# A convolution, mixer and MLP block on one core: the preparation in another order, and the last inverse transforms ahead of the mixing

## The chip, the cores and the metric

The kernel runs on one core of one Trainium2 chip. The time is that of one execution in microseconds on the device; the number given for a kernel is the median of its runs. The kernel before was run three times: 679.14 us, from 678.92 to 680.05. One further execution was profiled; its time is 679.21 us, and its span, from the first to the last instruction, 677.4 us. All times inside the kernel below come from that execution and count from the span's start.

## The reference, cut to what matters

The sequence has 2048 positions and 512 channels. A vector `c` gives six modulation vectors. Two residual parts follow, each behind a normalization and modulation:

```python
mod = (_silu(c) @ w_mod).reshape(c.shape[0], 6, 1, -1)      # sa, ca, ga, sb, cb, gb
h = _layernorm(x) * (1 + ca) + sa
x = x + ga * _A_ref(h, A_re, A_im, B_re, B_im, C_re, C_im, log_dt, Dskip)
h = _layernorm(x) * (1 + cb) + sb
x = x + gb * _B_ref(h, w1, w2, w3, w4)

# _A_ref: a state space convolution, 512 channels with 128 states each
logdA = exp(log_dt)[:, None] * (A_re + 1j * A_im)
K = einsum("dn,dnl,dn->dl", Cc, exp(logdA[:, :, None] * l), dB).real
y = irfft(rfft(pad(u)) * rfft(pad(K)))[:L] + u * Dskip

# _B_ref: token mixing by shifts, then an MLP
h = _gelu(_layernorm(x) @ w1);  hs = shifted(h, +1, -1, +2, -2) @ w2;  x1 = x + hs
return x1 + _gelu(_layernorm(x1) @ w3) @ w4
```

All is float32. Where the kernel multiplies matrices of full precision it splits a factor into a rounded part ("hi") and a rest ("lo") and adds up two or three products.

## The kernel before

The work of one core goes through five stages; their order on each engine is the order of the code, written out by hand (`manual_schedule`), and each engine works through its list in order. DMAs are issued by SP, GpSimd ("POOL") and at a few places by ScalarE ("ACT"), each queue in order as well.

**Preparation (0 to 31 us, lines 261 to 402).** From 128 x 512 inputs `ar`, `ai` (A), `br`, `bi`, `cr`, `ci` it makes the phases and weights of the kernel K. VectorE computes exp(log_dt) and silu's exponential in small operations (`exp_exact`, line 149, on `ld`, which holds log_dt and -c), then `la` and `tf`, the real and imaginary exponents (lines 319 to 322); `frac` takes a phase modulo one in two operations. `t64` is 64 times the phase (line 333). `hi` (line 309) is ScalarE's rounding into a slot of the tile `hilo`, `lo` (line 310) VectorE's rest. `place` (line 312) brings the rows of two such slots into matmul layout by TensorE and two ScalarE evictions: `TES` for the exponentials, `T0S` for the first phase. `parts` (line 360) does so for three pairs of slots into two PSUM tiles `px`, evicted as `T1S`. Lines 343 to 348 form the complex product C*B (`wr`, `wi`); lines 370 to 378 its phase by a quotient and ScalarE's Arctan; line 383 adds it to the phase, giving slots 4 and 5 of `hilo`. `exps(0, 0, 5)` (line 355) computes the first exponentials. GpSimd issues the loads of the tables PA, CE, C0, PB, C1 behind a copy that waits for `raw_ai` (line 286), then fills the constant tiles MG and ON (lines 291 to 299). SP loads the inputs, and behind VectorE's clearing of `DS` three modulation weights (1 MB each, `load_mod`) and two groups of u (1 MB each, `load_u`). At the end `wn` gets the weights of the states (lines 398 to 401). `mod_parts` (line 214) is the first half of a product c @ w_mod on TensorE with its eviction, `mod_sum` the second.

**Turns (31 to 205 us, lines 547 to 599).** For k = 0 to 31, `turns(k, cos)` (line 439) computes phases on TensorE into one of two PSUM tiles `xx`, 8 to 10 matmuls in pairs, and ScalarE takes the sine of them into `tr`. `products(k)` (line 459) multiplies them on VectorE with the exponentials, `burst(k)` (line 490) contracts over the states on TensorE. TensorE's order in step k: turns k+2, then burst k. The list `side` spreads other work over the steps: the statistics of u (`u_stats`), its normalization and its transform, and loads. For every fourth k the next exponentials come in between.

**Spectra (205 to 299 us, lines 1099 to 1152).** For sixteen steps the spectra of u and K are computed, multiplied, transformed back along one axis (`back`) and stored to a DRAM tile `ZT`.

**Last transforms and mixing (299 to 376 us, lines 1153 to 1294).** The second half of the channels has its last axis transformed from `ZT`. `load_inv(1, k)` loads block k, in halves or whole; `inv_half(1, g, i)` (line 725) is 16 small matmuls that yield one half of row group g, and returns the VectorE operation that adds it to the residual `X2`. The halves (3,1), (0,0), (3,0) and (0,1) need the blocks 0, 3, 4 and 7; (1,0), (1,1), (2,0), (2,1) the blocks 1, 2, 5 and 6. Those blocks live in a ring `ldp` of six buffers. Token mixing of eight groups of 256 rows begins with group 7: `first_stats`, `mix_mod1`, `mix_mod2` (VectorE and GpSimd), `mix_norm` (ScalarE), `transposed` (TensorE), `parts_of` (ScalarE evicts, VectorE forms the rest `nl`), `mix_half` (24 matmuls by W1, twice). `keep(n)` issues n matmuls whose result isn't used.

**Mixing and MLP (376 us to the end, `chan`).** TensorE works here without a break.

Of the kernel before, what the change touches and what calls it, by code (L numbers as in the profile page):

```python
# [82 lines left out]

def layouts(inp):
# [7 lines left out]
         "wm": np.ascontiguousarray(a("w_mod").reshape(4, 128, 6, 512).transpose(2, 1, 0, 3).reshape(6, 128, 2048)), "c": np.ascontiguousarray(a("c").reshape(4, 128).T),  # L92
         "ld": np.ascontiguousarray(perm(a("A_log_dt")).reshape(4, 128).T),
# [13 lines left out]
def body(ctx, tc, A):  # L107
# [15 lines left out]
    Y.dma_start(ident, A["ID"])  # L123
# [64 lines left out]
    T1S = ph.tile([128, 16, 128], F32R, name="T1S")  # L188
# [41 lines left out]
    ut = {}  # L230
# [33 lines left out]
    ld = pp.tile([128, 8], F32, name="ld")  # L264
    raw = {}
    PA = pp.tile([128, 2, 2, 128], F32R, name="PA")
    PB = pp.tile([128, 4, 4, 128], F32R, name="PB")
    cT = pp.tile([128, 4], F32, name="cT")
    cst = pp.tile([128, 512], F32, name="cst")
# [10 lines left out]
    with tc.manual_schedule():  # L280
        Y.dma_start(ld[:, :4], A["ld"])
        Y.dma_start(cT, A["c"])
# [8 lines left out]
        P.memset(cst, MAGIC)  # L291
        for r in (32, 96):
            P.memset(cst[r:r + 32], 1.0)
        P.tensor_copy(MG, cst)
        P.memset(cst[:, :384], 0.0)
        for i, (r, v) in enumerate(((0, 1.0), (0, -1.0), (32, 0.25))):
            for q in (r, r + 64):
                P.memset(cst[q:q + 1, i * 128:i * 128 + 128], v)
        P.tensor_copy(ON.rearrange("p a b -> p (a b)"), cst[:, :384])
# [33 lines left out]
        V.tensor_scalar(t64, tf, 64.0, None, op0=OP.mult)  # L333
        frac(t64, rr)
        hi(2, t64)
        place(TES, 6, PA)
        V.tensor_scalar(ex[:, 4:], ex[:, 4:], 1.0, None, op0=OP.add)
# [5 lines left out]
        V.tensor_mul(wr, cr, br)  # L343
# [21 lines left out]

        parts(range(4), 0)
        mp = [mod_parts(0)]
# [8 lines left out]
        V.tensor_mul(rc, rc, wi)  # L376
        V.scalar_tensor_tensor(t31, sg, 0.25, t31, op0=OP.mult, op1=OP.add)
        act(at0, rc, AF.Arctan)
        lo(2, t64)
        parts(range(4), 1)  # L380
# [3 lines left out]
        frac(at, t0)  # L384
        hi(4, at)
        mp[0]()
# [712 lines left out]
    with tc.manual_schedule():  # L1099
# [71 lines left out]
        for k, i in ((3, 1), (0, 0)):  # L1171
            load_inv(1, k, i, Y)
            load_inv(1, k + 4, i, Y)
# [141 lines left out]
```

## Time and profile before

| | |
|---|---|
| median of three runs | 679.14 us (678.92 to 680.05) |
| profiled execution: time, span | 679.21 us, 677.4 us |
| TensorE matmuls, busy | 633.1 us (93%) |
| VectorE busy | 496.8 us (73%) |
| ScalarE busy | 331.3 us (49%) |
| GpSimd busy | 118.4 us (17%) |
| first turns on TensorE | 31.67 us |
| first inverse half from the second `ZT` | 306.69 us |
| mean granted TensorE clock | 0.992 |

A timeline row reads: start in us, length in us, engine, line of the code, operation, written tile <- read tiles, shape, count, and in brackets the idle time of the engine just before and what ended it. PE is TensorE, PEld its weight loads, DVE VectorE, ACT ScalarE, POOL GpSimd, SPq the queue of SP. Line 115 is the helper through which every ScalarE operation goes, so ScalarE's rows are told apart by their tiles. Rows of the stage table have the busy time of each engine in a stretch, then the granted clock (1.00 is full), the busy share of the DMA engines and GB/s. Rows of the chain of waits have only start, length and what.

### The profile page before, as it was taken

The numbers are of one execution on the slowest core, as the hardware profiler recorded it, in microseconds if no ns is written. First come the engines' busy times: TensorE is split into PE (matmuls) and PEld (weight loads), VectorE is DVE, ScalarE is ACT, GpSimd is POOL, SyncE is SP. The second block draws the span as 40 slices with busy tenths as digits, with TensorE's granted clock in tenths as the row PEclk, the third lists the DMA queues.
The fourth block names the chain that finished last, engine by engine and source line by source line (L and its number), as shares of the span: only waits on it lengthen the run. The fifth ranks groups of instructions, "written<-read, shape, count | busy, mean of one in ns | idle before, by whom it ended". The sixth has DMA issues, their size and how long they took to land.

```text
span 677.4 us, 16876 instructions
## 1 busy us (share of the span) xinstructions
PE 633.1 (93%) x7195; PEld 507.1 (75%) x7195; DVE 496.8 (73%) x795; ACT 331.3 (49%) x505; POOL 118.4 (17%) x238
## 2 busy tenths in 40 slices
PE   1899999999999998968999999999999999999996
PEld 0456555665568877735889899898998989898895
DVE  7899999999996897997989777454674445363622
ACT  3978998898884665722446334022141213122121
POOL 4012212212207133203842002010010000000000
PEclk9999999999999999988999999999999999999999
DMA  8602274643838899966386010110100201010001
GB/s 306 287 2 75 75 229 107 202 124 80 296 64 311 289 372 354 364 209 197 110 268 237 1 60 4 49 46 16 48 31 25 70 16 48 1 62 1 1 32 31
DMA packets 50067, 86.42 MB, mean 128 GB/s; under 512 B 4676, under 2 KB 38472, under 8 KB 47400
## 3 DMA queue, kind: packets, MB, share of 16 engines
q1 hardware_dynamic: 45048, 60.97, 28.3%
q0 software_dynamic: 4624, 23.86, 9.7%
q8 instruction: 56, 0.92, 0.6%
q10 hardware_dynamic: 320, 0.52, 0.3%
q14 instruction: 19, 0.16, 0.1%
HBM read 59.12 MB, written 32.90 MB: 136 GB/s over the span
## 4 chain that ended last, share of the span: by engine, by line
PE 73%; DVE 4%; DMA 4%; issue 3%; ACT 2%; POOL 1%; SPq 0%; ACTq 0%; DVEq 0%; POOLq 0%
PE xx L448 7%; PE pm L840 7%; PE pm L838 7%; PE pm L837 7%; PE pa L957 6%; PE pa L956 6%; PE pa L964 6%; PE pk L679 4%; PE kp L498 4%; DMA ld<-ZT 3%; PE ph L894 2%; PE ph L895 2%; PE pu L426 2%; PE ph L897 2%; PE pz L701 2%
## 5 line engine op out<-in xcount | busy, mean ns | idle before, releaser
L115 ACT ACTIVATE gh<-pm 128x512 fp32r<-128x512 f32 (+1 forms) x48 | 26.9, 560 | 199.2 <-PE pm L840 199.2
L838 PE MATMUL pm<-nh,w3l 128*128 128x256 f32 (+1 forms) x352 | 85.6, 279 | 0.1
L837 PE MATMUL pm<-nh,w3h 128*128 128x256 f32 (+1 forms) x352 | 85.7, 278 | 0.0
L948 DVE TENSOR_TENSOR gl<-gf,gh 128x512 fp32r<-128x512 f32 (+1 forms) x48 | 30.8, 642 | 68.0 <-ACT gf L115 68.0
L956 PE MATMUL pa<-w4h,gh 128*128 128x512 f32 (+1 forms) x176 | 69.5, 395 | 0.0
L957 PE MATMUL pa<-w4l,gh 128*128 128x512 f32 (+1 forms) x176 | 68.9, 392 | 0.0
L838 PEld LDWEIGHTS pm<-nh,w3l 128*128 128x128 f32 (+1 forms) x352 | 65.2, 185 | 2.1 <-DVE w3l L757 0.5
L837 PEld LDWEIGHTS pm<-nh,w3h 128*128 128x128 f32 (+1 forms) x352 | 65.3, 186 | 1.4
L764 POOL TENSOR_TENSOR rs<-mv,eps_t 128x1 f32<-128x1 f32 (+1 forms) x39 | 11.0, 281 | 274.2 <-DVE mv L770 256.2
L840 PE MATMUL pm<-nl,w3h 128*128 128x256 f32 (+1 forms) x352 | 54.8, 277 | 0.1
L964 PE MATMUL pa<-w4h,gl 128*128 128x512 f32 (+1 forms) x176 | 48.0, 390 | 0.0
L449 PE MATMUL xx<-MG,ON 64*128 64x512 f32 x160 | 47.1, 390 | 0.0
L448 PE MATMUL xx<-MG,ON 64*128 64x512 f32 x160 | 47.0, 389 | 0.0
L840 PEld LDWEIGHTS pm<-nl,w3h 128*128 128x128 f32 (+1 forms) x352 | 46.6, 185 | 0.3 <-DVE nl L810 0.3
L900 DVE TENSOR_TENSOR h<-h,ph 128x512 f32<-128x512 f32 x16 | 11.0, 687 | 45.0 <-PE ph L897 45.0
L466 DVE SCALAR_TENSOR_TENSOR e<-tr,p 128x512 f32<-128x512 f32 x64 | 41.1, 683 | 0.4 <-ACT tr L115 0.4
L498 PEld LDWEIGHTS kp<-e,e 128*32 128x32 f32 x2048 | 30.1, 110 | 12.6 <-issue 7.9
L475 DVE TENSOR_TENSOR e<-tr,p 128x1024 f32<-128x1024 f32 x32 | 39.0, 1218 | 0.0
L476 DVE TENSOR_TENSOR e<-tr,m 128x1024 f32<-128x1024 f32 x32 | 39.0, 1218 | 0.0
L115 ACT ACTIVATE p<-xx 128x1024 f32<-128x1024 f32 (+1 forms) x40 | 37.5, 980 | 2.1 <-PE xx L252 0.5
L964 PEld LDWEIGHTS pa<-w4h,gl 128*128 128x128 f32 (+1 forms) x176 | 33.0, 188 | 7.1
L115 ACT ACTIVATE tr<-xx 128x1024 f32<-128x1024 f32 x32 | 33.0, 1030 | 9.7 <-PE xx L449 7.4
(241 smaller groups left out, 1709.7 us busy)
## 6 DMA issues: line engine op xcount, KB each, us to landing
VU<-vs SPq DMA_DIRECT2D x64, 128.0 KB, 3.4
ld<-VU SPq DMA_DIRECT2D x16, 512.0 KB, 8.7
ZT<-z POOLq DMA_DIRECT2D x30, 256.0 KB, 6.3
Dw<-in_w POOLq DMA_DIRECT2D x8, 688.0 KB, 4.7
xu<-in_u SPq DMA_DIRECT2D x4, 1024.0 KB, 11.9
KX<-in_x POOLq DMA_DIRECT2D x4, 1024.0 KB, 8.6
ld<-ZT SPq DMA_DIRECT2D x8, 512.0 KB, 10.4
win<-GD SPq DMA_DIRECT2D x32, 128.0 KB, 2.5
```

The source lines that it names most:

```text
L115: return S.activation(out, in_, f, bias=bias, scale=scale)
L448: T.matmul(x[:, :512], la, ma, start=(i == 0), stop=(i == len(ops) - 1))
L449: T.matmul(x[:, 512:], lb, mb, start=(i == 0), stop=(i == len(ops) - 1))
L466: V.scalar_tensor_tensor(e0[:, 1, a], tr[:, 1, 0], 1.0 - 2.0 * a, mg[:, a], op0=OP.mult, op1=OP.mult)
L475: V.tensor_mul(e0[:, 0], tr[:, 0, 0:1].to_broadcast([128, 2, 512]), mg)
L498: T.matmul(kp[32 * j:32 * j + 32, (k % 2) * 4 + g], e1[:, r, d], e0[:, r, :, d * 32:d * 32 + 32], start=(r == 0), stop=(r == 1), skip_grou ...
L837: T.matmul(p, wh[:, k, c], hi[k], start=(k == 0), stop=False)
L838: T.matmul(p, wl[:, k, c], hi[k], start=False, stop=False)
L840: T.matmul(p, wh[:, k, c], lo[k], start=False, stop=(k == 3))
L956: T.matmul(acc[i], gh[:m, e, s], W4h[:m, f], start=(f == 0), stop=False)
L957: T.matmul(acc[i], gh[:m, e, s], W4l[:m, f], start=False, stop=False)
L964: T.matmul(acc[i], gl[:m, e, s], W4h[:m, f], start=False, stop=(f == 10))
```

## The change

In the preparation:

- log_dt, c (twice) and four columns of constants come as one tile `lc` by one load, first in SP's queue; the load of `ident` goes from the very first place to behind u's first group.
- MG and ON are spread from these columns by ScalarE; GpSimd's fills and casts are gone.
- GpSimd's loads of the tables wait for `raw_ar` instead of `raw_ai`. A second copy on GpSimd waits for `wr`, then GpSimd (not VectorE) clears `DS`, behind which SP's large loads stand. Their order is now modulation 0, u 0, ident, modulation 1 and 2, u 1.
- `t64` is formed on ScalarE. The products `wr`, `wi` stand ahead of `frac(t64)`; the rest `lo(0)` and the place step for T0S go behind the quotient and Arctan; the first two `parts` are issued together; silu's three small operations go behind `frac(at)`.
- T1S is two tiles, each evicted by one operation. `mod_parts(1)` goes from ahead of the first turns to behind turns (0,1), `mod_sum` 0 and 1 behind turns (1,0), the transposes of `wn` ahead of turns (0,1).
- The statistics of u's first two blocks go from step 0 of the turns to the preparation, one ahead of and one behind the four operations on `wn`.

In the last transforms:

- Two of the first four loads of blocks go to ScalarE's queue.
- Blocks 1 and 5 of the second half get two buffers of their own (`xb`); the PSUM pool `psy` has four buffers instead of two.
- The halves (1,0), (1,1), (2,0) stand on TensorE right behind (0,1), (2,1) behind the addition of (0,0), all ahead of the transposes of group 7; `keep(14)` becomes `keep(4)`. The additions on VectorE keep their places.

```diff
+def constant_columns():
+    c = np.zeros((2, 64, 4), np.float32)
+    c[:, :32, 0], c[:, 32:, 0] = MAGIC, 1.0
+    c[:, 0, 1], c[:, 0, 2], c[:, 32, 3] = 1.0, -1.0, 0.25
+    return c.reshape(128, 4)
...
-    Y.dma_start(ident, A["ID"])
...
-    T1S = ph.tile([128, 16, 128], F32R, name="T1S")
+    T1S = [ph.tile([128, 8, 128], F32R, name=f"T1S{i}") for i in range(2)]
...
-        Y.dma_start(ld[:, :4], A["ld"])
-        Y.dma_start(cT, A["c"])
+        Y.dma_start(lc, A["ld"])
         for k in raw:
             Y.dma_start(raw[k].rearrange("p t n -> p (t n)"), A[k])
+        act(MG, lc[:, 12:13].to_broadcast([128, 512]))
+        act(ON, lc[:, 13:16, None].to_broadcast([128, 3, 128]))
         gate = pp.tile([128, 4], F32, name="gate")
-        P.tensor_copy(gate[:, 0:1], raw["ai"][:, 0, 0:1])
+        P.tensor_copy(gate[:, 0:1], raw["ar"][:, 0, 0:1])
...
-        P.memset(cst, MAGIC)
...
-        P.tensor_copy(ON.rearrange("p a b -> p (a b)"), cst[:, :384])
...
-        V.memset(DS, 0.0)
-        for j in range(4):
-            Y.dma_start(DS[32 * j:32 * j + 1], A["dk"][j:j + 1])
-        load_mod(0)
-        load_mod(1)
-        load_mod(2)
-        load_u(0)
-        load_u(1)
-        hi(0, tf)
-        lo(6, la)
-        V.tensor_scalar(t64, tf, 64.0, None, op0=OP.mult)
-        frac(t64, rr)
-        hi(2, t64)
-        place(TES, 6, PA)
-        V.tensor_scalar(ex[:, 4:], ex[:, 4:], 1.0, None, op0=OP.add)
-        V.reciprocal(ex[:, 4:], ex[:, 4:])
-        V.tensor_mul(scb, ex[:, 4:], cT)
...
+        hi(0, tf)
+        act(t64, tf, scale=64.0)
+        lo(6, la)
+        place(TES, 6, PA)
         V.tensor_mul(wr, cr, br)
...
+        P.tensor_copy(gate[:, 1:2], wr[:, 0:1])
+        P.memset(DS, 0.0)
+        for j in range(4):
+            Y.dma_start(DS[32 * j:32 * j + 1], A["dk"][j:j + 1])
+        load_mod(0)
+        load_u(0)
+        Y.dma_start(ident, A["ID"])
+        load_mod(1)
+        load_mod(2)
+        load_u(1)
...
-        lo(0, tf)
...
+        frac(t64, t0)
+        hi(2, t64)
         act(t31, tf, scale=31.5)
         exps(0, 0, 5)
         act(ws[:, :1], hpi, AF.Sin)
-        place(T0S, 0, PA)
...
-        parts(range(4), 0)
-        mp = [mod_parts(0)]
...
+        lo(0, tf)
         V.scalar_tensor_tensor(t31, sg, 0.25, t31, op0=OP.mult, op1=OP.add)
         act(at0, rc, AF.Arctan)
+        place(T0S, 0, PA)
         lo(2, t64)
-        parts(range(4), 1)
+        parts(range(4), 0, 1)
...
         frac(at, t0)
+        V.tensor_scalar(ex[:, 4:], ex[:, 4:], 1.0, None, op0=OP.add)
+        V.reciprocal(ex[:, 4:], ex[:, 4:])
+        V.tensor_mul(scb, ex[:, 4:], cT)
         hi(4, at)
-        mp[0]()
+        mp = [mod_parts(0)]
         lo(4, at)
         parts((0, 1), 2, 3)
         parts((2, 3), 2, 3)
-        mp.append(mod_parts(1))
         act(wn, at0, AF.Sin, scale=-1.0, bias=hpi)
-        T1v = T1S.rearrange("p (t v) n -> p v t n", v=4)
+        act(ws, at0, AF.Sin)
+        mp[0]()
         for i in range(2):
-            act(T1v[:, i], px[0].rearrange("p (v t n) -> p v t n", v=2, t=4)[:, i])
-        act(ws, at0, AF.Sin)
-        act(T1v[:, 2:], px[1].rearrange("p (v t n) -> p v t n", v=2, t=4))
-        mp[1]()
+            act(T1S[i].rearrange("p (t v) n -> p v t n", v=2), px[i].rearrange("p (v t n) -> p v t n", v=2, t=4))
+        ul[0] = ln_stats(ph, [ut[0][:, 0]], "l0")
...
+        ul[1] = ln_stats(ph, [ut[0][:, 1]], "l1")
...
         turns(0, 0)
-        turns(0, 1)
         wps = psu.tile([128, 512], F32, name="pu")
...
         act(WN, wps)
+        turns(0, 1)
+        mod_parts(1)()
+        turns(1, 0)
         ms = [mod_sum(n) for n in range(2)]
-        turns(1, 0)
...
-        psy = a2.enter_context(tp("psy", 2, space=PSUM, side="right"))
+        psy = a2.enter_context(tp("psy", 4, space=PSUM, side="right"))
+        xb = a2.enter_context(tp("xb", 2))
+        for k in (1, 5):
+            zis[1, k] = xb.tile([128, 4, 256], F32, name="xb")
...
         for k, i in ((3, 1), (0, 0)):
             load_inv(1, k, i, Y)
-            load_inv(1, k + 4, i, Y)
+            load_inv(1, k + 4, i, S)
...
         a01 = inv_half(1, 0, 1, psw, "pm")
-        keep(14)
+        a10 = inv_half(1, 1, 0, psy, "py")
+        a11 = inv_half(1, 1, 1, psy, "py")
+        a20 = inv_half(1, 2, 0, psy, "py")
+        keep(4)
...
         a00()
+        a21 = inv_half(1, 2, 1, psy, "py")
         mix_norm(7)
...
-        a10 = inv_half(1, 1, 0, psy, "py")
-        a11 = inv_half(1, 1, 1, psy, "py")
...
-        a20 = inv_half(1, 2, 0, psy, "py")
...
-        a21 = inv_half(1, 2, 1, psy, "py")
```

More of the change, by code (lines that the diff above doesn't have):

```diff
@@ L91, in layouts @@
          "x": np.ascontiguousarray(u.reshape(32, 4, 4, 2048).transpose(2, 1, 0, 3).reshape(4, 128, 2048)),
-         "wm": np.ascontiguousarray(a("w_mod").reshape(4, 128, 6, 512).transpose(2, 1, 0, 3).reshape(6, 128, 2048)), "c": np.ascontiguousarray(a("c").reshape(4, 128).T),
-         "ld": np.ascontiguousarray(perm(a("A_log_dt")).reshape(4, 128).T),
+         "wm": np.ascontiguousarray(a("w_mod").reshape(4, 128, 6, 512).transpose(2, 1, 0, 3).reshape(6, 128, 2048)), "ld": np.ascontiguousarray(np.concatenate([perm(a("A_log_dt")).reshape(4, 128).T] + [a("c").reshape(4, 128).T] * 2 +
+                                                   [constant_columns()], 1)),
          "dk": np.ascontiguousarray(a("A_Dskip").reshape(2, 2, 2, 64).transpose(0, 2, 1, 3).reshape(4, 128)),
@@ L228, in mod_sum @@
         return lambda: act(mods[k], m)
-    ut = {}
+    ut, ul = {}, {}
     def load_u(g):
@@ L263, in body @@
     pp = pr.enter_context(pool("prep"))
-    ld = pp.tile([128, 8], F32, name="ld")
+    lc = pp.tile([128, 16], F32, name="lc")
+    ld, cT = lc[:, :8], lc[:, 8:12]
     raw = {}
@@ L267, in body @@
     PB = pp.tile([128, 4, 4, 128], F32R, name="PB")
-    cT = pp.tile([128, 4], F32, name="cT")
-    cst = pp.tile([128, 512], F32, name="cst")
     hilo = pp.tile([128, 8, 512], F32R, name="hilo")
@@ L290, in body @@
         Y.dma_start(FU, A["FU"].rearrange("p (a b) -> p a b", a=2))
-        P.memset(cst, MAGIC)
[L292 to L298, printed above, removed]
-        P.tensor_copy(ON.rearrange("p a b -> p (a b)"), cst[:, :384])
         Y.dma_start(FK, A["FK"])
@@ L406, in body @@
     uv = a1.enter_context(pool("uv", bufs=2, reuse_waits="tile"))
-    ul = {}
     def u_stats(b):
@@ L442, in turns @@
         r1 = slice(64 - r0.start, 128 - r0.start)
-        l0, l1, c = T0S[r0, t], T1S[r1, t * 2 + k % 2], slice(k % 2 * 512, k % 2 * 512 + 512)
+        l0, l1, c = T0S[r0, t], T1S[t % 2][r1, t // 2 * 2 + k % 2], slice(k % 2 * 512, k % 2 * 512 + 512)
         x = psx.tile([128, 1024], F32, name="xx")
@@ L519, in body @@
     for i in range(16):
-        side[max(at(i) - 2, 0)].append(lambda i=i: u_stats(i))
+        if i > 1:
+            side[max(at(i) - 2, 0)].append(lambda i=i: u_stats(i))
         side[at(i)].append(lambda i=i: u_norm(i))
```

## The prediction

> **What bounds the kernel now.** I read the page first (chain of waits, busy shares), then the busy time by stages, then the timelines of the two places that the change touches. The page's chain by engine, and three rows by stage (length, busy time of TensorE, weight loads, VectorE, ScalarE, GpSimd, granted clock, DMA share, GB/s):
>
> ```profile
> PE 73%; DVE 4%; DMA 4%; issue 3%; ACT 2%; POOL 1%; SPq 0%; ACTq 0%; DVEq 0%; POOLq 0%
> ...
> 10.00:20.00 10.00, 4.73 (x11) 2.66 (x12) 9.59 (x18) 6.02 (x10) 3.48 (x10) 1.00 1.07 419
> ...
> 190.00:200.00 10.00, 10.00 (x188) 6.69 (x186) 10.00 (x12) 7.78 (x11) 0.00 (x0) 1.00 0.16 35
> ...
> 318.00:345.00 27.00, 25.76 (x238) 22.29 (x238) 25.34 (x51) 13.07 (x21) 18.04 (x49) 1.00 0.39 128
> ```
>
> The preparation (0 to 31 us) hangs on VectorE, 9.59 of 10 us busy, and at its end on ScalarE. In the turns (31 to 205) TensorE and VectorE are both full, so two chains run abreast and the later one counts. In the mixing (318 to 345) VectorE is busy 25.34 of 27. Later the work is TensorE's, so a shift that reaches it reaches the end.
>
> **The change, part by part: the preparation.** Timeline rows (start, length, what), VectorE and ScalarE:
>
> ```profile
> 1.65 0.43 SPq L282 DMA_DIRECT2D cT<-in_c  x1
> ...
> 3.33 0.17 DVE L301 TENSOR_SCALAR ld<-cT 128x4 f32<-128x4 f32 x1 [1.95 <-DMA cT<-in_c]
> ...
> 7.04 0.63 ACT L115 ACTIVATE hilo<-tp_la 128x512 fp32r<-128x512 f32 x1 [5.02 <-DVE tp_la L319]
> ...
> 9.39 0.71 DVE L333 TENSOR_SCALAR tp_t<-tp_tf 128x512 f32<-128x512 f32 x1
> ...
> 11.78 0.15 DVE L337 TENSOR_SCALAR dt_o<-dt_o 128x4 f32<-128x4 f32 x1
> ...
> 12.26 0.69 DVE L343 TENSOR_TENSOR tp_wr<-raw_cr,raw_br 128x512 f32<-128x512 f32 x1
> ...
> 17.09 0.69 DVE L370 TENSOR_TENSOR tp_mc<-raw_cr,raw_br 128x512 f32<-128x512 f32 x1
> 17.48 1.92 ACT L115 ACTIVATE p<-xx 128x1024 f32<-128x1024 f32 x2
> ...
> 24.53 0.68 DVE L377 SCALAR_TENSOR_TENSOR tp_rr<-tp_la,tp_rr 128x512 f32<-128x512 int32 x1
> ...
> 25.10 0.63 ACT L115 ACTIVATE tp_at<-tp_rc 128x512 f32<-128x512 f32 x1
> ...
> 25.62 1.06 ACT L115 ACTIVATE C0N<-C 128x1024 fp32r<-128x1024 f32 x1
> ...
> 26.57 0.63 ACT L115 ACTIVATE C1N<-C 128x512 fp32r<-128x512 f32 x1
> ...
> 27.68 0.63 ACT L115 ACTIVATE hilo<-tp_at 128x512 fp32r<-128x512 f32 x1 [0.48 <-DVE tp_at L278]
> ```
>
> TensorE's rows of the same stage:
>
> ```profile
> 10.70 2.05 PE L316 MATMUL pu<-hilo,PA 128*128 128x512 f32 x4 [10.70 <-DMA PA<-in_PA]
> ...
> 21.67 1.91 PE L316 MATMUL pu<-hilo,PA 128*128 128x512 f32 x4
> ...
> 23.38 1.77 PE L363 MATMUL xx<-hilo,PB 128*128 128x512 f32 x4
> ...
> 28.36 2.38 PE L363 MATMUL xx<-hilo,PB 128*128 128x512 f32 x8 [1.08 <-ACT hilo L115]
> ...
> 30.67 1.06 PE L218 MATMUL pu<-KX,scb 128*32 128x512 f32 x8
> ...
> 31.67 0.50 PE L448 MATMUL xx<-C,T0S 64*128 64x512 f32 x1
> ...
> 39.57 1.06 PE L218 MATMUL pu<-KX,scb 128*32 128x512 f32 x8 [0.46 <-ACT modu L115]
> 40.57 0.49 PE L448 MATMUL xx<-C,T0S 64*128 64x512 f32 x1
> ```
>
> Start: the small inputs are one transfer, first on SP's queue where cT was the third (1.65). VectorE's 3.33 becomes about 2.43: 0.9 saved.
>
> VectorE to the products: the scaling by 64 (0.71) goes to ScalarE, the rounding behind it (to 11.78) and the three small ones (11.78 to 12.26) move back, the clearing of DS (under 0.1) goes to GpSimd. The first product moves from 12.26 to 12.26 - 0.9 - 2.87 - 0.1 = 8.4. From there to the maximum lay 4.83 with one remainder; now six products and the rounding (two of about 0.55), 5.2: the maximum starts at 13.6 instead of 17.09.
>
> ScalarE: the spread of MG and ON (0.63 and some 0.5) lies in its wait of 5.02 ahead of 7.04, with over 2 us to spare. PA is asked for when raw_ar, not raw_ai, has come, some 1.5 us earlier; the place step that waited for it (10.70) then ends near 11.2, and TES, the three copies, hi and t31 fill ScalarE until about 14.8. This order has no slack: PA later than 9.1 delays all behind it one to one. The exponentials and the table load took 17.48 to 25.10 with two T0S evictions in it (about 1.0), which now come behind: 14.8 + 6.6 = 21.4 to 21.5 for Arctan; VectorE has the quotient at 13.6 + 7.4 = 21.05. Then 0.63 Arctan, T0S (its matmuls wait for the moved remainder, 21.8 to 23.7, by 1.91), C0N and C1N (1.5 from start to next): hi(4) at 25.8 instead of 27.68. VectorE's own chain would have it at 24.8; the three small operations lie there for nothing, and cost 0.5 if ScalarE were quicker.
>
> Then two sines, one eviction, and a whole T1S half by one operation (by the like 128x1024 row, 1.06): the first turns at 29.15 instead of 31.67. TensorE no longer does the second mod_parts ahead of them, but behind; the transposes of wn now stand ahead of the second half turn, and wait: the last remainder ends at 27.1, one u statistic (0.8, below), four products at 0.69 each, 30.6; TensorE is free about 1.0 after 29.15, so it waits 0.6. From the first turn to the third (31.67 to 40.57) were 8.90, with 0.46 and some 0.4 idle; now one mod_parts more (1.06), the wait of 0.6, those idles gone: 9.6. The third turn comes at 38.75, **1.8 earlier**.
>
> VectorE gains more:
>
> ```profile
> 39.55 0.69 DVE L142 BATCH_NORM_STATS2 lus<-xu 128x6 f32<-128x512 f32 x1
> ...
> 41.16 1.26 DVE L466 SCALAR_TENSOR_TENSOR e<-tr,p 128x512 f32<-128x512 f32 x2
> ...
> 188.09 1.04 ACT L115 ACTIVATE tr<-xx 128x1024 f32<-128x1024 f32 x1
> ...
> 189.16 1.29 DVE L466 SCALAR_TENSOR_TENSOR e<-tr,p 128x512 f32<-128x512 f32 x2
> ```
>
> Two statistics (39.55 to 41.16, 1.6) leave its way, so it is 2.5 to 4.1 ahead. But at 189.16 its product starts 0.03 after the sine (188.09 + 1.04) that it needs: by then the chain of TensorE and ScalarE leads, and of it only 1.8 is saved.
>
> TensorE's clock: four L363 took 1.77 at 23.38, eight took 2.38 at 28.36: it was slow after a pause. Now TensorE pauses before the second place step (21.8), has sixteen L363 and a mod_parts behind it, and ScalarE wants the first eight plus four and mod_parts by 28.05. If the quick rate comes at 25.7, four after the pause as before, they end at 28.6, still covered by the wait for wn; if at 28, they cost 1.0. I take 0.1. So the preparation is worth **-1.7**, between -3.0 (VectorE alone) and -0.6. The Trainium skill (TensorE: Matmul & The Clock Gate, part 1) has the clock doubled only after one fully busy free-running window of about 3.4 us; by that rule the quick rate comes 3.4 to 6.8 after 21.8, and the sum would be -0.6 to -1.8 by the window's phase. The trace's change from 1.77 for four to 2.38 for eight agrees with such a step.
>
> The large loads now wait for wr, some 2 us later than before. The queue is full anyway (419 GB/s); u's first group passes two of the modulation's, and needs to be there by 27.1.
>
> **The last spectra and transforms.** A row of the chain, rows by stage, a wait of SP's queue, and timeline rows:
>
> ```profile
> 300.93 0.42 SPq L720
> ```
>
> ```profile
> 306.00:307.00 1.00, 0.31 (x4) 0.23 (x8) 0.00 (x0) 0.00 (x0) 0.00 (x0) 0.50 1.06 367
> ...
> 311.00:312.00 1.00, 1.00 (x20) 0.61 (x16) 1.00 (x2) 0.00 (x0) 0.92 (x3) 0.71 0.43 133
> ```
>
> ```profile
> SPq L720 <- PE pm L730: 4.8, 1, 4.8
> ```
>
> ```profile
> 306.69 3.64 PE L730 MATMUL py<-ld,FI 128*32 128x256 f32 x32 [8.01 <-DMA ld<-ZT]
> 310.08 2.66 PE L730 MATMUL pm<-ld,FI 128*32 128x256 f32 x32
> 312.67 3.47 PE L1169 MATMUL pT<-w1h 128*128 128x512 f32 x14
> ...
> 317.88 0.88 PE L802 MATMUL pT<-ident,h 128*128 128x128 f32 x6 [0.75 <-ACT h L115]
> 318.69 1.93 PE L730 MATMUL py<-ld,FI 128*32 128x256 f32 x32
> ```
>
> ```profile
> 319.83 1.28 DVE L810 TENSOR_TENSOR nl<-pT,nh 128x512 fp32r<-128x512 f32 x2
> ...
> 327.67 1.29 DVE L810 TENSOR_TENSOR nl<-pT,nh 128x512 fp32r<-128x512 f32 x2 [0.30 <-ACT nh L115]
> ```
>
> Two queues: the fourth load is issued about 0.9 earlier, but the issue of 256 KB takes 0.42 and its move 0.7 or more at 367 GB/s, so the data, not the issue, ends last. Bounds 0 and -0.9; I take 0, because what follows no longer hangs on it. The Trainium skill (Trainium Kernel Development and Optimization, Key Constraints) says that several issuing engines save only the issue time, their transfers interleaving on the same DMA engines. By it the term is 0 as well, and the third load of SP's queue now competes with the two on ScalarE's.
>
> Transforms ahead: all four halves need k = 1, 2, 5 and 6. Two of those loads waited 4.8 us for TensorE to free their buffers. With the two new buffers they follow the others at once: the earlier 3 MB ended near 311.5 (133 GB/s in that us), 1 MB more at 367 is 2.9, so they land near 314.3. TensorE, done at 312.7, waits; three halves at 0.97 (1.93 for two) end at 317.2, four keeps at 0.25 at 318.2, the fourth half at 319.15. The transposes of group 7 stand behind all this on TensorE: they were at 317.88 and end now near 320.2. ScalarE's eviction and VectorE's nl wait behind them: nl at 320.35 instead of 319.83. VectorE then has 0.5 less, and gets back its later wait of 0.30 (327.67), since the third and fourth half no longer lie between. VectorE's additions keep their places, so the 3.9 us that TensorE sheds are not on its way. **+0.2**; bounds -0.8 (loads early by 1) and +3.2 (below). The extra banks and buffers cost nothing, as their earlier users end before 299.
>
> Sum: -1.7 + 0.2 = -1.5 on the profiled run's 679.21 (span 677.4, 1.81 around it) is 677.7; the median, 679.14, lies 0.07 lower: **677.6**.
>
> **Rivals.** (1) *VectorE alone sets the turns*: TensorE and ScalarE catch up. Against it stands the 0.03 at 189.16; for it that both are full. -3.0 + 0.2: 676.3. (2) *TensorE stays slow through the preparation*: quick only at 28 or later, -0.7 + 0.2: 678.6. For it the slow row at 23.38. The Trainium skill's clock-gate rule, named above, gives this for a late window. (3) *The fillers aren't free*: u's first group or PA lands late and the statistic holds up wn, by 1.1, -0.6 + 0.2: 678.7; it is the case that the change doesn't do what it says. (4) *Slower*: TensorE's clock falls in the new pause from 312.7 to 314.3, as it did behind the pause before 306 (0.50 at 306, back only after 311). The three halves then cost 1.97 each (3.64 for two) and everything is 3.0 later at the transposes: -1.7 + 3.2, 680.6. It decides once nl of group 7 comes later than 321.5, at full clock when the loads land after 315.7. Against it: the pause is 1.6 us, the one that slowed it was 8.01.
>
> **How the numbers follow.** Forecast 0.42, (1) 0.10, (2) 0.19, (3) 0.11, (4) 0.18. No change means within 0.2% (1.36 us), about what this kernel's measurement can tell: 677.8 to 680.5. The forecast lies just below it; three quarters of its chance are faster, with (1) and a little of (2) 0.45. (4) gives 0.18 slower, the rest 0.37. The range goes from (1) to (4): 676.0 to 680.8; the forecast's own is 677.0 to 678.3.
>
> **What would show it.** Right: VectorE's first operation near 2.4, hi(4) near 25.8, the first turn near 29.2 to 29.7, the third near 38.8; TensorE's wait for the last loads near 314 (less 1.8), clock unbroken, nl half a us late. Wrong: the first turn later than 30.5 with L363 at 0.44 each (2); VectorE waiting for u (3); clock 0.50 after the pause (4); stage boundaries at 205 earlier by 2.5 or more (1).

## The result and the profile after

The changed kernel takes 684.78 us (median of six runs, 682.05 to 686.39) where the kernel before takes 679.21 beside it (678.35 to 680.76): a ratio of 1.0076, 95% interval 1.0059 to 1.0092. It is slower by 0.76%, and the forecast, 677.6, was wrong in its sign. The profiled execution of after took 685.41 us, with a span of 683.6 against 677.4.

Where the 6.2 us of span come from is seen from the same moments in both timelines (start in us; the operations named are those of the prediction):

| moment | before | after | difference |
|---|---|---|---|
| ScalarE's hi(4) | 27.68 | 25.91 | -1.77 |
| first turn on TensorE | 31.67 | 30.84 | -0.83 |
| third turn, turns(2, 0) | 40.57 | 40.32 | -0.25 |
| last product of step 7 | 77.83 | 77.09 | -0.74 |
| last product of step 8 | 83.58 | 83.68 | +0.10 |
| last product of step 31, end of the turns | 204.20 | 205.20 | +1.00 |
| last `back`, ScalarE's z | 295.38 | 296.45 | +1.07 |
| first last transform on TensorE | 306.69 | 306.67 | -0.02 |
| nl of group 7 | 319.83 | 325.37 | +5.54 |
| third nl | 337.80 | 343.33 | +5.53 |
| fourth nl | 345.75 | 352.13 | +6.38 |

So there are four places: the preparation, a loss in the turns, a gain at the first loads, and the large loss between 307 and 325, with a smaller one behind it.

The preparation, VectorE and ScalarE in the timeline of after:

```profile
2.45 0.17 DVE L298 TENSOR_SCALAR lc<-lc 128x4 f32<-128x4 f32 x1 [1.07 <-DMA lc<-in_ld]
...
14.04 0.69 DVE L361 TENSOR_TENSOR tp_mc<-raw_cr,raw_br 128x512 f32<-128x512 f32 x1 [0.55 <-ACT raw_br L122]
...
21.64 0.63 ACT L122 ACTIVATE tp_at<-tp_rc 128x512 f32<-128x512 f32 x1
...
25.91 0.62 ACT L122 ACTIVATE hilo<-tp_at 128x512 fp32r<-128x512 f32 x1
```

These four answer to 3.33, 17.09, 25.10 and 27.68 of before. VectorE's chain came as predicted, to 0.1 at hi(4), which was forecast at 25.8; the maximum, forecast at 13.6, is 0.4 late (it waits 0.55 for ScalarE). TensorE in the same stage:

```profile
22.26 1.65 PE L313 MATMUL pu<-hilo,PA 128*128 128x512 f32 x3 [2.49 <-DVE hilo L307]
23.71 3.62 PE L357 MATMUL xx<-hilo,PB 128*128 128x512 f32 x8
27.25 1.35 PE L224 MATMUL pu<-KX,scb 128*32 128x512 f32 x8
28.53 2.11 PE L357 MATMUL xx<-hilo,PB 128*128 128x512 f32 x8
30.84 0.50 PE L440 MATMUL xx<-C,T0S 64*128 64x512 f32 x1 [0.20 <-ACT T1S L122]
```

Each L357 group is eight matmuls of one shape. Behind a pause of 2.49 us they take 3.62, without one 2.11. The trace's own record of the granted clock has its first entry, full clock, at 27.88, just behind the slow group. The first turn therefore starts at 30.84, not at the 29.15 forecast.

The turns, one row by stage of before and two of after (length, busy time of TensorE, weight loads, VectorE, ScalarE, GpSimd, granted clock, DMA share, GB/s):

```profile
72.00:76.00 4.00, 3.66 (x17) 1.88 (x17) 3.85 (x7) 3.79 (x5) 0.34 (x1) 1.00 0.00 0
...
72.00:76.00 4.00, 3.66 (x16) 1.97 (x16) 3.85 (x8) 3.77 (x5) 1.01 (x2) 0.96 0.00 0
76.00:80.00 4.00, 4.00 (x80) 2.78 (x78) 3.43 (x6) 3.71 (x5) 1.35 (x4) 0.62 0.51 176
```

In after the clock falls to a half for 3.4 us in the middle of a full stage. In before it stays at 1.00 behind the same 3.66 us of busy time.

The last transforms, rows by stage and then the timeline of after:

```profile
312.00:313.00 1.00, 0.53 (x12) 0.05 (x4) 1.00 (x2) 0.00 (x0) 0.17 (x1) 1.00 1.08 345
313.00:314.00 1.00, 0.00 (x0) 0.00 (x0) 0.93 (x4) 0.00 (x0) 0.00 (x0) 1.00 1.16 364
314.00:315.00 1.00, 0.00 (x0) 0.00 (x0) 0.97 (x3) 0.00 (x0) 0.81 (x2) 0.80 0.59 189
315.00:316.00 1.00, 0.00 (x0) 0.00 (x0) 0.97 (x3) 0.20 (x1) 0.84 (x5) 0.50 0.08 17
316.00:317.00 1.00, 0.00 (x0) 0.00 (x0) 0.93 (x4) 0.62 (x2) 0.91 (x4) 0.50 0.06 17
317.00:321.00 4.00, 3.94 (x40) 2.14 (x44) 2.87 (x6) 0.81 (x1) 1.41 (x4) 0.50 0.00 0
```

```profile
306.67 3.64 PE L724 MATMUL py<-ld,FI 128*32 128x256 f32 x32 [6.92 <-DMA ld<-ZT]
...
317.06 0.64 PE L724 MATMUL py<-ld,FI 128*32 128x256 f32 x2 [4.53 <-DMA ld<-ZT]
...
321.92 1.20 PE L1167 MATMUL pT<-w1h 128*128 128x512 f32 x4
...
324.05 1.09 PE L796 MATMUL pT<-ident,h 128*128 128x128 f32 x8
...
325.37 1.29 DVE L804 TENSOR_TENSOR nl<-pT,nh 128x512 fp32r<-128x512 f32 x2 [5.47 <-ACT nh L122]
```

TensorE stands still from 312.5 to 317.06, waiting for blocks 1, 2, 5 and 6. The bulk of them is there within the us from 314, about when it was forecast (314.3), but at 315 and 316 there is still a trickle of 17 GB/s at a DMA share of 0.08 and 0.06 (one of 16 engines would be 0.06), and the transforms wait for its end: the last load lands at 316.93. Meanwhile the clock goes to 0.50; the three halves end at 321.9, 4.9 us after their start, instead of in 2.9. VectorE waits 5.47 for nl, where before it did not wait at all.

### The profile page after: what moved, and what is told of

The parts are those of the page before. It is cut to its first block, busy times and chain, and to the rows that moved or that the text cites. A ratio compares the mean times of both kernels' runs of the same rounds, so it can differ in the third digit from the quotient of the medians.

```text
span 683.6 us, 16844 instructions
## 1 busy us (share of the span) xinstructions
PE 635.9 (93%) x7185; PEld 508.1 (74%) x7185; DVE 495.9 (73%) x793; ACT 333.3 (49%) x507; POOL 113.2 (17%) x228
## 4 chain that ended last, share of the span: by engine, by line
PE 76%; DMA 4%; DVE 4%; issue 2%; ACT 2%; POOL 1%; SPq 1%; ACTq 0%; DVEq 0%; POOLq 0%
PE xx L440 8%; PE pm L834 7%; PE pm L832 7%; PE pm L831 7%; PE pa L950 6%; PE pa L951 6%; PE pa L958 6%; PE pk L673 4%; PE kp L490 4%; PE pz L695 2%; DMA ld<-ZT 2%; PE pu L418 2%; PE pk L619 2%; PE pk L643 2%; PE ph L889 2%
## 5 line engine op out<-in xcount | busy, mean ns | idle before, releaser
L440 PE MATMUL xx<-MG,ON 64*128 64x512 f32 x160 | 48.0, 396 | 0.0
L441 PE MATMUL xx<-MG,ON 64*128 64x512 f32 x160 | 48.0, 396 | 0.0
L673 PEld LDWEIGHTS pk<-VK,xu 64*64 64x64 f32 x768 | 33.0, 133 | 6.5 <-issue 5.7
```

Of the source, the lines that this page charges most:

```text
L440: T.matmul(x[:, :512], la, ma, start=(i == 0), stop=(i == len(ops) - 1))
L441: T.matmul(x[:, 512:], lb, mb, start=(i == 0), stop=(i == len(ops) - 1))
L673: T.matmul(p[gh][kk * 64:kk * 64 + 64, i, ro], w, VK[jh][rows, ri * 32 + k1].rearrange("p j g -> p (j g)"), start=(ri == 0), stop=(ri == 1 ...
```

## The experiments

The time of every kernel below is a median of 6 to 12 runs, and its ratio, with a 95% interval, is to the kernel before on the same chip. The parts of the change are taken one by one, then the clock.

**Only the preparation.** After, with the lines of the last transforms put back to those of before.

```diff
-        psy = a2.enter_context(tp("psy", 4, space=PSUM, side="right"))
-        xb = a2.enter_context(tp("xb", 2))
...
+        psy = a2.enter_context(tp("psy", 2, space=PSUM, side="right"))
...
-            load_inv(1, k + 4, i, S)
+            load_inv(1, k + 4, i, Y)
...
-        keep(4)
+        keep(14)
```

The two tiles of `xb` are gone with it, and the halves a10, a11, a20 and a21 stand in their old places.

> Only the preparation (with the order of the first turns) is taken over; the last transforms are those of before. Theory 1 (the loss sits in the last transforms: TensorE's pause for the late loads and the slow clock behind it): the third turn comes near 40.3 instead of 40.57 as in the profile of after, so 678.9, ratio 0.9996. Theory 2 (the fall of the clock at 75 to 79, seen in the profile of after, belongs to the new preparation): about 1 us lost in the turns each time, 680.0, ratio 1.001, and a granted clock below 1 between 60 and 100. My prediction's step, -1.7, would give 677.5.

Measured: 679.01 us, ratio 0.9992 (0.9977 to 1.0007). First turn 31.14, third turn 40.61: nothing is gained there, since the eight L357 took 3.62 again. The clock also fell in the turns (0.59 from 76 to 80). So far both theories hold; the next kernel parts them.

**Only the last part.**

```diff
-        psy = a2.enter_context(tp("psy", 2, space=PSUM, side="right"))
+        psy = a2.enter_context(tp("psy", 4, space=PSUM, side="right"))
+        xb = a2.enter_context(tp("xb", 2))
...
-            load_inv(1, k + 4, i, Y)
+            load_inv(1, k + 4, i, S)
...
-        keep(14)
+        a10 = inv_half(1, 1, 0, psy, "py")
+        a11 = inv_half(1, 1, 1, psy, "py")
+        a20 = inv_half(1, 2, 0, psy, "py")
+        keep(4)
...
         a00()
+        a21 = inv_half(1, 2, 1, psy, "py")
```

This is the kernel before with the lines of the last transforms taken from after.

> Only the last part is taken over (two queues, two more buffers and banks, four half transforms ahead of the mixing); the preparation is that of before. Theory 1: the first transform 1.1 earlier by the faster loads, then the split of group 7 (nl, 319.83 before) 5.5 later by pause and clock, and 0.8 more by the clock near 345: 679.2 + 4.4 to 5.2 = 683.6 to 684.4, ratio 1.007. Theory 2: half of the loss or less sits here, 682 or below. My prediction's step, +0.2, would give 679.4.

Measured: 683.71 us, ratio 1.0070 (1.0047 to 1.0093). Nearly the whole loss sits here. The clock fell at the same place in the turns, with the preparation of before. The row by stage of this kernel:

```profile
76.00:80.00 4.00, 4.00 (x68) 2.84 (x70) 4.00 (x6) 3.57 (x6) 1.69 (x3) 0.61 0.48 176
```

Theory 2 falls: in the 13 profiles of this study the clock falls within the turns in four (after, these two, and the one with half sets below), and not in the other nine, six of which have the new preparation. With the old preparation it falls in one of four, this one. So the new preparation isn't what it takes; that it comes rather by the execution than by the kernel fits this, but no kernel was profiled twice. It costs 0.9 to 1.3 us: from the third turn to the end of the turns the shift against before goes from -0.25 to +1.00 in after, from +0.04 to +1.31, from +0.01 to +0.92 and from -0.99 to +0.35 in the others. What sets it off I did not find. All four lie right behind a stretch in which the next exponentials are computed (in after eight matmuls of TensorE from 72.22 to 74.82, then a pause of 0.34), but before has the same stretch, with the same busy time, and keeps its clock.

**The halves back in their old places**, the rest of the change kept.

```diff
-        a10 = inv_half(1, 1, 0, psy, "py")
-        a11 = inv_half(1, 1, 1, psy, "py")
-        a20 = inv_half(1, 2, 0, psy, "py")
-        keep(4)
+        keep(14)
...
-        a21 = inv_half(1, 2, 1, psy, "py")
```

The four halves follow in their old places.

> After, with the four half transforms back behind the transposes of group 7 and the 14 keeping matmuls back; the two queues, the two buffers, the four banks and the preparation stay. Theory 1: no pause for the loads of blocks 1, 2, 5 and 6, the clock stays at 1 from 312 on, and the 1.1 that the two queues gain at the first loads stays in part: 679.2 - 0.3 - 1.1 = 677.8, ratio 0.998. A rival, that the two queues or the earlier loads themselves disturb (by sharing the DMA engines with the first loads): 680 or above.

Measured: 677.43 us, ratio 0.9971 (0.9955 to 0.9987). Putting four transforms back turns +0.76% into -0.29%: 0.0105 of the time, 7.1 us, is the price of standing ahead. Timeline:

```profile
304.69 3.64 PE L724 MATMUL py<-ld,FI 128*32 128x256 f32 x32 [6.62 <-DMA ld<-ZT]
...
317.85 1.28 DVE L804 TENSOR_TENSOR nl<-pT,nh 128x512 fp32r<-128x512 f32 x2
```

From the first transform to nl of group 7 it is 13.16 here and 18.70 in after (325.37 - 306.67): 5.5 more. With the 0.85 that after loses up to the fourth nl the two traces account for 6.4 of the 7.1.

**The pause filled.** After, with `keep(18)` ahead of the three halves.

```diff
+        keep(18)
         a10 = inv_half(1, 1, 0, psy, "py")
```

> After, with 18 more keeping matmuls (0.25 each, 4.5 in all) on TensorE in front of the half transforms that wait for the late loads, so that its clock isn't let down in the pause. If the clock is a cost of its own: the three halves take 0.97 instead of 1.6 each, the transposes of group 7 come at 322.0 instead of 324.05, and 682.5 to 683.0 follows, ratio 1.005. If the late loads are the whole cost and the clock is none: 684.8, ratio 1.008.

Measured: 681.54 us, ratio 1.0037 (1.0020 to 1.0054). Work whose result is thrown away makes the kernel faster by 0.0039, 2.6 us. Timeline:

```profile
311.00 4.38 PE L1167 MATMUL pT<-w1h 128*128 128x512 f32 x18
315.31 0.41 PE L724 MATMUL py<-ld,FI 128*32 128x256 f32 x2
...
321.50 1.29 DVE L804 TENSOR_TENSOR nl<-pT,nh 128x512 fp32r<-128x512 f32 x2 [3.40 <-ACT nh L122]
```

The clock stays up, and the three halves take 2.7 (315.31 to 318.04, where the four keeping matmuls follow). From the first transform (304.87) to nl it is 16.63. Of the 5.5, then, 3.5 is the wait for the loads and the order, and 2.0 the clock. The clock's part is that of one execution: in the kernel with only the last part the same distance is 17.58 (322.85 - 305.27), 0.95 more than here. There the slow clock lasted 3.4 us, in after 6.8. The clock still fell later, as in after and in the kernel with only the last part. The row by stage of this one:

```profile
340.00:344.00 4.00, 3.73 (x17) 3.53 (x18) 3.90 (x10) 0.00 (x0) 1.75 (x6) 0.60 0.83 256
```

**Only two queues and buffers.** Before, with nothing but these lines:

```diff
-            load_inv(1, k + 4, i, Y)
+            load_inv(1, k + 4, i, S)
-        psy = a2.enter_context(tp("psy", 2, space=PSUM, side="right"))
+        psy = a2.enter_context(tp("psy", 4, space=PSUM, side="right"))
+        xb = a2.enter_context(tp("xb", 2))
+        for k in (1, 5):
+            zis[1, k] = xb.tile([128, 4, 256], F32, name="xb")
```

> Before, with only the two issuing queues, the two buffers and the four banks; preparation and order of the transforms are those of before. If the gain of the kernel with the halves put back (677.43) comes from the loads: the first transform near 305.3 instead of 306.69 and nl of group 7 near 318.3 instead of 319.83, so 679.5 - 1.5 = 678.0, ratio 0.9975. If two queues save only issue time, as my prediction had it (0): 679.5, ratio 1.000, and the gain was the preparation's.

Measured: 677.77 us, ratio 0.9974 (0.9962 to 0.9986), the first theory. This is the gain hidden in the change, and the kernel with the halves put back owes its time to it. The chain of waits, first of before, then of this kernel (start, length, what):

```profile
300.93 0.42 SPq L720
...
301.47 5.08 DMA ld<-ZT
306.56 0.14 issue
306.69 0.61 PE py L730
```

```profile
300.02 0.44 ACTq L720
300.46 0.04 issue
300.50 4.96 DMA ld<-ZT
305.46 0.04 issue
305.50 1.50 PE py L730 x11
```

The last of the four loads takes about 5.0 us from its issue in both (5.08 and 4.96); it is issued 0.97 earlier, and the transform starts 1.19 earlier (306.69 - 305.50). Queue and buffers were not timed apart; the chain puts the earlier start down to the queue.

**The clock ahead of the first transform.** The kernel with the halves put back, with 30 keeping matmuls there instead of 6.

```diff
-        keep(6)
+        keep(30)
         inv_half(1, 3, 1, psy, "py")()
```

> The kernel with the halves put back (two queues, buffers and preparation of after), and in front of the first transform 30 keeping matmuls instead of 6, so that TensorE works until about 304 while it waits for the first loads. If the clock after a pause is a cost of its own on the path: granted clock 1 from 300 to 312, the two halves x32 in 1.93 instead of 3.64, VectorE's first addition 0.9 earlier, 677.4 - 1.0 = 676.4, ratio 0.9955 to before. If the loads alone set the pace there: 677.4, ratio 0.997.

Measured: 675.63 us, ratio 0.9948 (0.9934 to 0.9962). Timeline:

```profile
303.68 1.93 PE L724 MATMUL py<-ld,FI 128*32 128x256 f32 x32 [1.42 <-DMA ld<-ZT]
...
306.82 1.93 PE L724 MATMUL pm<-ld,FI 128*32 128x256 f32 x32 [1.20 <-DMA ld<-ZT]
...
315.97 1.28 DVE L804 TENSOR_TENSOR nl<-pT,nh 128x512 fp32r<-128x512 f32 x2
```

The first group takes 1.93 instead of 3.64; from its start to nl of group 7 it is 12.29 instead of 13.16, 0.9 less, as expected. The rest of the 1.6 us between the two medians' ratios isn't told apart from the scatter, and the two intervals (0.9934 to 0.9962, 0.9955 to 0.9987) overlap a little: the 0.9 rests on the trace.

**The clock in the preparation.** The kernel with the halves put back, with six matmuls more (result unused) between the exponentials and the place step.

```diff
+        for _ in range(6):
+            T.matmul(px[0][:, :512], PA[:, 0, 0], hilo[:, 6], start=True, stop=True)
```

> The kernel with the halves put back, and in the preparation six matmuls more (result unused) on TensorE between the exponentials and the place step of T0S, so that TensorE doesn't pause from 19.8 to 22.3. If the slow TensorE is what took the preparation's gain (term of 0.1 in my prediction): eight L357 in 1.8 instead of 3.3 to 3.6, the first turn at 29.2 to 29.6 instead of 30.3 to 31.1, third turn near 38.7, and 1.3 less at the end if the rest follows: 676.1, ratio 0.995. If the spectra take up what the turns gain, as the last back step of the two kernels that came late out of the turns suggests: third turn the same 38.7, but 677.0 to 677.4, ratio 0.997.

Measured: 676.53 us, ratio 0.9949 (0.9933 to 0.9966). TensorE in the timeline, with the six matmuls first:

```profile
19.33 2.92 PE L354 MATMUL xx<-hilo,PA 128*128 128x512 f32 x6
...
23.70 2.00 PE L359 MATMUL xx<-hilo,PB 128*128 128x512 f32 x8
...
29.16 0.49 PE L442 MATMUL xx<-C,T0S 64*128 64x512 f32 x1 [0.21 <-ACT T1S L122]
...
39.04 0.50 PE L442 MATMUL xx<-C,T0S 64*128 64x512 f32 x1
```

Eight matmuls in 2.00 instead of 3.33 in the kernel it is built on (3.62 in after), the first turn at 29.16 where the prediction had 29.15, the third at 39.04 where it had 38.75. The preparation alone, held against the kernel with two queues only, is now worth 0.9949 - 0.9974 = -0.0025, 1.7 us; without these six matmuls it is 0.9971 - 0.9974 = -0.0003. The intervals overlap here as well, so the moments of the trace carry this more than the times do.

**Half sets.** The kernel with 30 keeping matmuls; blocks 1, 2, 5, 6 loaded in halves, those for (1,0) and (2,1) first, and these two transforms ahead of the mixing with `keep(6)`.

```diff
-        for k in (1, 2):
-            load_inv(1, k)
-            load_inv(1, k + 4)
+        for s in range(2):
+            for k, i in ((1, s), (2, 1 - s)):
+                load_inv(1, k, i)
+                load_inv(1, k + 4, i)
...
+        a10 = inv_half(1, 1, 0, psy, "py")
+        a21 = inv_half(1, 2, 1, psy, "py")
+        keep(6)
```

> As the kernel with 30 keeping matmuls, and two half transforms ahead of the mixing in the place of 8 of the 14 keeping matmuls: blocks 1, 2, 5 and 6 are loaded in halves, those halves first that these two transforms need (1 MB instead of 2 has to land, near 311). If moving transforms ahead is worth something once their loads are there: 1 to 2 us less than the kernel with 30 keeping matmuls, 675. If they were hidden behind the wait for nl of group 7 anyway: the same as it, 676.4. If the wait remains (a tail of the loads later than 312): slower by as much as TensorE waits.

Measured: 678.28 us, ratio 0.9983 (0.9972 to 0.9994). A row by stage, then rows of the timeline:

```profile
336.00:340.00 4.00, 4.00 (x23) 4.00 (x24) 3.86 (x10) 1.38 (x3) 1.71 (x7) 0.60 0.97 300
```

```profile
316.57 1.28 DVE L804 TENSOR_TENSOR nl<-pT,nh 128x512 fp32r<-128x512 f32 x2
...
334.55 1.26 DVE L804 TENSOR_TENSOR nl<-pT,nh 128x512 fp32r<-128x512 f32 x2
343.36 1.29 DVE L804 TENSOR_TENSOR nl<-pT,nh 128x512 fp32r<-128x512 f32 x2 [0.78 <-ACT nh L122]
```

From VectorE's first addition (305.42) to nl of group 7 it is 11.15; in the kernel with the 30 keeping matmuls (304.82 to 315.97) it is 11.15 too. In before it is 11.14 (308.69 to 319.83). So VectorE's own chain sets that nl as long as TensorE is ready in time: even where TensorE doesn't wait 4.5 us for loads, transforms ahead gain nothing there. They cost later: from the third nl to the fourth it is 8.81 instead of 7.95 (341.91 - 333.96), because TensorE's clock falls (0.60 in the row by stage from 336 to 340). The whole distance of the two kernels, 0.0035 or 2.4 us, is more than this; where the rest comes from isn't settled.

**Both measures on the clock.** The kernel with the halves put back, with

```diff
+        for _ in range(6):
+            T.matmul(px[0][:, :512], PA[:, 0, 0], hilo[:, 6], start=True, stop=True)
...
-        keep(6)
+        keep(30)
```

> After, with the halves put back, 30 keeping matmuls in front of the first transform and the six matmuls more in the preparation: the two measures on TensorE's clock together. If their gains are independent (each about 0.0022 of the time beyond the kernel with the halves put back, 0.9971): ratio 0.9925, 674.4. If the loads between take the preparation's part: 0.9945, 675.7.

Measured: 675.05 us, ratio 0.9945 (0.9928 to 0.9962): the fastest by a little, but not separable from either measure alone. Third turn 38.91, end of the turns 202.80, last z 293.46; the kernel with the 30 keeping matmuls alone had 39.49, 203.25 and 293.52. The 0.45 gained at the end of the turns is 0.06 at the last back step, so the second case is the one that the traces bear out.

**The clock ahead of the first transform, with one queue.** Before, with

```diff
-        keep(6)
+        keep(34)
         inv_half(1, 3, 1, psy, "py")()
```

> Before, with 34 keeping matmuls in front of the first transform instead of 6 and nothing else. If the slow clock behind the wait for the first loads costs as much with one queue: the first x32 group in 1.93 instead of 3.64, VectorE's first addition 0.9 earlier, 679.5 - 1.0 to 1.5 = 678.0 to 678.5, ratio 0.998. If with one queue the second pair of loads comes too late for it to matter: ratio 1.000.

Measured: 678.12 us, ratio 0.9991 (0.9975 to 1.0007): not told apart from no change. Timeline:

```profile
305.33 1.93 PE L730 MATMUL py<-ld,FI 128*32 128x256 f32 x32 [1.04 <-DMA ld<-ZT]
...
309.02 1.93 PE L730 MATMUL pm<-ld,FI 128*32 128x256 f32 x32 [1.76 <-DMA ld<-ZT]
...
317.61 1.28 DVE L810 TENSOR_TENSOR nl<-pT,nh 128x512 fp32r<-128x512 f32 x2
```

The first group is quick, but the second waits 1.76 us for its loads; with two queues it could begin 3.14 behind the first (306.82 - 303.68), here 3.69. That wait doesn't reach nl of group 7: from VectorE's first addition (306.46) to it there are 11.15 us, as with two queues, and from the first transform it is 12.28 instead of 13.14 in before. So the trace has the 0.9 of the first case; in time the interval leaves both open. The clock differs between the runs of this one kernel: nine of the twelve show a mean granted clock of 0.998 to 1.000 and take 676.77 to 678.31, three show 0.992 to 0.994 and take 678.56, 681.05 and 681.70.

**The moved work done again in its old place.** The kernel with `keep(18)`, which computes (2,0) and (2,1) a second time, unused.

```diff
+        inv_half(1, 2, 0, psy, "py")
         mix_half(0, hl, 0)
...
         hl = parts_of(transposed(mh.pop(1)[0]))
+        inv_half(1, 2, 1, psy, "py")
```

> The kernel with 18 keeping matmuls more, and the half transforms (2,0) and (2,1) computed once more, with their result unused, at the two places from which the change took them. It does more work and nothing less. If TensorE's clock falls near 340 to 348 because the moved transforms left pauses there (granted clock 0.60 to 0.66 in all four kernels with the halves ahead, 1.00 in the others): the clock stays at 1 there, the fourth nl comes 8.0 behind the third as in before (345.75 - 337.80) instead of 8.8, and 681.5 - 0.8 = 680.7, ratio 1.0025. If that fall has another cause: 681.5 or more, ratio 1.0037 or above.

Measured: 681.06 us, ratio 1.0021 (1.0008 to 1.0034). A row by stage and rows of the timeline:

```profile
340.00:344.00 4.00, 3.07 (x24) 2.66 (x23) 3.90 (x9) 0.11 (x1) 1.81 (x8) 1.00 0.60 181
```

```profile
340.49 1.25 DVE L804 TENSOR_TENSOR nl<-pT,nh 128x512 fp32r<-128x512 f32 x2
348.43 1.25 DVE L804 TENSOR_TENSOR nl<-pT,nh 128x512 fp32r<-128x512 f32 x2
```

The clock stays at 1.00 and the fourth nl follows in 7.94, as in before. In all four traces with halves ahead and no work in their old place the clock falls here (0.60 to 0.66), in this one profile it doesn't: the pauses left by the moved transforms let it down. In time the two intervals (1.0021 and 1.0037) overlap, though the 0.0016 between them, 1.1 us, is of the expected size.

## Why the prediction was wrong, point by point

- **VectorE's chain in the preparation: right.** hi(4) at 25.91 for 25.8.
- **"I take 0.1" for TensorE's clock in the preparation: the first step that failed.** The pause before the second place step was named, and so was rival (2), but most of the L357 behind it were priced at the quick rate. They took 2.82 to 3.62 in the seven profiles with the new preparation and no extra matmuls, where a filled pause gave 2.00 and 2.40. The term -1.7 was -0.25 at the third turn of after, and +0.04 to -1.08 in the other six (mean of the seven -0.6). The cause is shown, not only argued: with the pause filled the forecast moments come to 0.0 and 0.3. In the seven, the first entry of the granted clock, full clock, stands between 25.68 and 28.11, in after at 27.88; the eight take 2.82 with the earliest and 3.62 with the three latest. The prediction priced 28 at 1.0 and held 25.7 to be covered; but at 25.68 the third turn came at 39.49 for 38.75. A slip in the sum is small beside this: from the first turn to the third its terms add up to 9.7, not 9.6. The Trainium skill (TensorE: Matmul & The Clock Gate, Part 1) was quoted with a range of -0.6 to -1.8 by the phase of the window; by its rule, as an estimate, the quick rate comes 3.4 to 6.8 us after the pause. The trace agrees in after, where TensorE works without a break from 22.26 and the full clock stands at 27.88, 5.6 later; in the seven it is 3.2 to 5.6, once a little under the rule's 3.4. The mean, -0.6, is that range's lower end.
- **The shift of the third turn reaches the end of the turns: right,** where the clock doesn't fall between: the shifts against before at the two moments are -0.77 and -0.66, -0.52 and -0.38, -0.66 and -0.52, -1.08 and -0.95, -1.53 and -1.36, -1.66 and -1.40 in the six such profiles. VectorE's larger lead is lost, as argued from the 0.03 at 189.16; rival (1) did not happen, nor did (3): u's first statistic ran at 27.16 without a wait. PA did come late, TensorE waiting for it until 9.77, after the 9.1 that was named; but the exponentials started at 14.95 for 14.8, so "one to one" was too strict.
- **"Later the work is TensorE's, so a shift that reaches it reaches the end": too simple.** The stage from the end of the turns to the last z took 91.2 us in before and 89.6 to 92.2 in the twelve other profiles, with the same code in each. A gain of half a us from the turns can vanish there, and a loss of 1.3 did (204.20 and 205.51 at the end of the turns, 295.38 and 295.23 at the last z). Why it varies stays open.
- **Two queues, "I take 0": wrong, at the bound named.** I let the moving data end last. The chain shows that the last of the four lands about 5.0 us after its issue with one queue and with two, so 0.97 of earlier issue is 0.97 of earlier data and more. The Trainium skill's sentence that issuing from several engines saves only issue time (Trainium Kernel Development and Optimization, Key Constraints) agrees with this; it was my reading that issue time was worth nothing that failed. In time the term is -1.8 (-0.0026), issue and buffers together.
- **Transforms ahead, "+0.2": the step that decided.** Three parts failed. The loads' landing was taken from the mean rate: the bulk was there within the us from 314, as forecast, but the last load landed at 316.93, 2.6 later. Rival (4), the clock in the pause, had the right mechanism and the right threshold (nl later than 321.5, loads later than 315.7), and was given 0.18 because the pause would be 1.6 us; it was 4.5. And its price, 3.0, held only the pause's clock: at nl it was +5.5, 3.5 for the wait and 2.0 for the clock. (A half at 1.97 was also too slow for 3.64 for two; the three took 4.92, 1.64 each.) Third, "the 3.9 us that TensorE sheds are not on its way" was right about time and missed what the work did: it kept the clock up. Its absence cost 0.85 at the fourth nl (6.38 - 5.53). The 0.30 that VectorE was to get back did not come either: it waits 0.28 at the second nl of after (333.20).
- **The sum.** The preparation alone (-0.0008) and the last part alone (+0.0070) add up to +0.0062, inside the interval of the 0.0076 measured. Within the last part the queues and buffers are -0.0026, which leaves +0.0096, 6.5 us, for the transforms ahead, where I had +0.2 us.

## What to carry to other kernels

When work is moved ahead of a wait, ask when its last byte lands, not when the mean rate would be through, and what stands behind it on an engine that works in order. On TensorE, a filler in a wait and work that isn't on the path are both worth something: in this kernel matmuls with unused results gained 0.39% in the large pause and some 0.2% (with overlapping intervals) in two smaller ones, and useful work taken out of a thin stretch lost 0.9 us. A change of several parts is best timed part by part: here a gain of 0.26% lay under a loss of 1%.

## What the runs showed of the hardware that was not expected

- The clock falls without a still engine. In the turns it fell in four profiles behind a stretch in which TensorE was busy 3.66 of 4 us, a stretch that other profiles pass at full clock; so the busy time doesn't tell the two apart. At 345 in after it fell behind a thin stretch rather than a long pause; the longest pause there is 1.50 us (4.53 in the fall at 314):

```profile
342.00:343.00 1.00, 0.54 (x5) 0.34 (x3) 0.97 (x2) 0.00 (x0) 1.00 (x3) 1.00 0.92 313
343.00:344.00 1.00, 0.00 (x0) 0.00 (x0) 0.97 (x4) 0.00 (x0) 0.92 (x4) 1.00 0.00 0
344.00:345.00 1.00, 0.86 (x5) 0.66 (x6) 1.00 (x2) 0.00 (x0) 0.72 (x3) 1.00 0.47 163
345.00:346.00 1.00, 1.00 (x9) 1.00 (x8) 0.97 (x3) 0.00 (x0) 0.00 (x0) 0.66 0.92 241
```

- In the clock records of the 13 traces every slow stretch that begins and ends between the preparation and the last 7 us lasts 3.41 us or two or three times as much (6.83, 10.24): 3.41 for each fall in the turns, 6.83 behind the pause before 317 in after, 3.41 at the same place in the kernel with only the last part. A pause's price therefore comes in steps.
- A batch of loads can end with a tail at a small part of the rate: 17 GB/s at a DMA share of 0.08 and 0.06, 2 us long in after, and shorter or hardly there in the other profiles. Why the last packets come so late wasn't found.
- The granted clock in the rows by stage reads 1.00 all through the preparation, where the same eight matmuls take 3.62 or 2.00 us by what stood ahead of them. The record of the clock has no entry ahead of the first one at 23.58 to 28.11. Until then the slow rate is read from the durations, not from that column.
